# A normalised block of x made from a column layout instead of TensorE turns

## The chip, the core and the metric

The kernel runs on one core of one Trainium2 chip. A core has five engines that run side by side, each through its own list of instructions in order: TensorE (PE) multiplies matrices and turns tiles, VectorE (DVE) and GpSimd (POOL) do elementwise work and reductions, ScalarE (ACT) does functions of one argument and copies, SyncE (SP) issues transfers. Transfers (DMAs) are issued from the queues of SP, ACT and POOL and move data between device memory and the on-chip memory SBUF, which has 128 partitions. TensorE writes into PSUM, eight banks of 128 partitions by 512 float32. The metric is the device time of the whole program in microseconds (us); lower is better.

## The reference

x is 2048 tokens by 512 features, float32. It is normalised per token, and two branches start from the normalised xn: attention with 32 heads of 16, and a gated feed-forward network of width 1792.

```python
m = mean(x, axis=-1); v = var(x, axis=-1)
xn = (x - m) / sqrt(v + 1e-5)
q, k, v = split(xn @ wqkv)                    # 32 heads of 16
s = merge(softmax(q @ k.T * 16**-0.5) @ v) @ wo
f = (silu(xn @ w_gate) * (xn @ w_up)) @ w_down
out = x + s * silu(f)
```

Mean and variance belong to a token, that is, to a row of x. The products with wqkv, w_gate and w_up sum over features, and TensorE sums over partitions, so xn is needed with its features on the partitions and its tokens along the row.

## The kernel before

The tokens are worked in four blocks of TB = 512 (b = 0 to 3), each of NT = 4 tiles of 128 tokens; the features are DT = 4 chunks of 128. Float32 products are made from two halves: a tile is split into a high half, rounded to the matmul's type, and a low half, the remainder, and a product is high x high + low x high + high x low. So a tile of a projection is 12 matmuls: 4 chunks by 3 products.

The program has a prologue and a main part. The prologue makes xn in halves (`xt`, two buffers, used in turn by even and odd blocks), projects q, k and v for all tokens, and stores them in device memory (`q_d`, `k_d`, `v_d`), with the halves of xn (`xt_d`). The main part reads them back and runs attention and the feed-forward network as one stream of matmuls, their order laid out ahead of time by a planner (`plan`), then the output projection. There is no synchronisation between the parts but the data itself.

The order of the prologue is written out by hand: a loop over b, and in it over 12 tiles of projections, n = 0 to 11 (L765 to L869). Block 0 starts with the four value tiles (`value_tile`, one for 128 tokens) and goes on with the eight feature tiles (`feature_tile`, one for 128 features of q or k); the other blocks do the feature tiles first. Around each tile the loop issues what other engines are to do meanwhile for the next block. Instructions of one engine run in the order in which the loop issues them, so an instruction that waits holds up all that stand behind it on its engine.

What the change touches:

- `load_x` (L542) loads the next block of x, four transfers on SP of 128 tokens each, into `xin`, which is the tile `facc` of the main part. It is issued at n = 2 in block 0 and at n = 1 later.
- `stats` (L607) makes mean and variance of one tile of 128 tokens on DVE, tokens on the partitions. `rates` (L617) makes 1/sqrt(v + eps) for four tiles: a square root on ACT, and small DVE instructions that end with L628. They are issued behind the tiles n = 2 to 5.
- `norm` (L630) makes xn of a tile with one DVE instruction, at n = 6 to 9.
- `turn_x` (L652) turns it, at n = 7 to 10: four transposes on TensorE (L638) into the PSUM bank `acc` or `extra`, a cast on ACT to the high half (L647), a subtraction on DVE for the low half (L650). Behind the fourth tile, POOL issues two transfers of 1 MB that store the halves in `xt_d` (L656).

What runs beside it in the same steps: each feature tile has a square (L722) and a cast (L723) on ACT, a subtraction on DVE (L724), a running maximum on DVE outside block 0 (L728) and a store of 512 KB on SP (L726), with four buffers for its PSUM bank and four for its halves. In steps 3 to 18 ACT also copies parts of block 0's halves for the main part (L763). In block 0 the weights of the projections still arrive: a load on SP five tiles ahead (L565), a cast on ACT two tiles ahead (L573), a subtraction on POOL right after (L577). Each tile of block 0 needs its weights' halves.

Of the kernel before, what the change touches and what calls it, by code (L numbers as in the profile page):

```python
# [9 lines left out]
F32 = mybir.dt.float32  # L10
# [9 lines left out]
P = 128  # L20
# [5 lines left out]
NB = 4  # L26
TB = S // NB
NT = TB // P
DT = D // P
# [87 lines left out]


@with_exitstack
def tile_block(ctx: ExitStack, tc: tile.TileContext, x, wqkv, wo, w_gate, w_up, w_down, out):  # L120
    nc = tc.nc
    ctx.enter_context(tc.manual_schedule())
    x, out = x[0], out[0]
    mm, act, dve, sp, pool = nc.tensor.matmul, nc.scalar.activation, nc.vector, nc.sync, nc.gpsimd

    dram = ctx.enter_context(tc.tile_pool(name="dram", bufs=1, space=DRAM))
# [4 lines left out]
    xt_d = dram.tile([NB, 2, P, DT, TB], F32, name="xt_d")  # L131
    g_d = dram.tile([S, D], F32, name="g_d")
    o_d = dram.tile([DT, NB, P, TB], F32, name="o_d")
    s_d = dram.tile([1, TB], F32, name="s_d")

    const = ctx.enter_context(tc.tile_pool(name="const", bufs=1))
    one = ctx.enter_context(tc.tile_pool(name="one", bufs=1))
# [3 lines left out]
    ident = const.tile([P, P], F32, name="ident")  # L141
# [188 lines left out]
    rows = [slice(t * P, (t + 1) * P) for t in range(S // P)]  # L330
# [179 lines left out]
    begin, n = [], 0  # L510
# [10 lines left out]
    with ExitStack() as pro:  # L521
        pc = pro.enter_context(tc.tile_pool(name="pc", bufs=1))
# [6 lines left out]
        extra = pex.tile([P, 512], F32, name="extra")  # L529
        turns = acc, extra  # L530

        xin = facc
        wide = [slice(i * D // 2, (i + 1) * D // 2) for i in range(2)]

        def load_tile(t):
            if t:
                sp.dma_start(xin[:, t % NT], x[t * P:(t + 1) * P])
            else:
                for engine, w in zip((nc.scalar, sp), wide):
                    engine.dma_start(xin[:, t, w], x[t * P:(t + 1) * P, w])  # L540

        def load_x(b):  # L542
            for t in range(NT):
                load_tile(b * NT + t)

        load_tile(0)
        busy = pc.tile([P, P], F32, name="busy")
        dve.memset(busy, 0.0)
# [54 lines left out]
        rs = pc.tile([P, NT], F32, name="rs")  # L603
        nw = pc.tile([P, NT], F32, name="nw")
        xn = {}

        def stats(t):  # L607
            st = p2.tile([P, 2, dve.BN_STATS_DIM], F32, tag="st", name="st")
            if t or xn:
                dve.bn_stats(st[:, 0], xin[:, t])  # L610
                dve.bn_aggr(mv[:, t], st[:, 0])
            else:
                for i, w in enumerate(wide):
                    dve.bn_stats(st[:, i], xin[:, t, w])
                dve.bn_aggr(mv[:, t], st)

        def rates(first, last):  # L617
            r, n = (i[:, first:last] for i in (rs, nw))
            act(n, mv[:, first:last, 1], AF.Sqrt, bias=root, scale=4.0)
# [3 lines left out]
            dve.reciprocal(r, n)  # L623
            for t in range(first, last):
                h, n1, v1 = (i[:, t:t + 1] for i in (rs, nw, ve))
                dve.tensor_scalar(n1, v1, h, h, op0=ALU.mult, op1=ALU.mult)
            for w in cols:
                dve.scalar_tensor_tensor(rs[:, w], nw[:, w], 3.0, rs[:, w], op0=ALU.add, op1=ALU.mult)  # L628

        def norm(t, columns=(slice(0, D),)):  # L630
            xn[t] = two.tile([P, D], F32, tag="ga", name="xn")
            for w in columns:
                made = dve.tensor_scalar(xn[t][:, w], xin[:, t, w], mv[:, t, 0:1], rs[:, t:t + 1],
                                         op0=ALU.subtract, op1=ALU.mult)
            return made
# [15 lines left out]

        def turn_x(b, t, between=None):  # L652
            split_x(b, t, turn(t), between)
            if t == NT - 1 and b:
                for j in range(2):
                    pool.dma_start(xt_d[b, j], xt[b % 2][j].bitcast(F32))  # L656


        def project(pairs, xh, xl, tokens, order=None, ps=None):
# [98 lines left out]
        def copy_fx(i):  # L758
# [3 lines left out]
            dst = fx[halves[h], j].rearrange("p (c u) t -> u p c t", u=2)[u]  # L762
            nc.scalar.copy(dst[:, 2 * w:2 * w + 2], xt[0][j][halves[u], 2 * w:2 * w + 2])  # L763

        for b in range(NB):  # L765
            more = b + 1 < NB
            slots = [(feature_tile, m) for m in range(8)]
            slots = [(value_tile, t) for t in range(NT)] + slots if b == 0 else slots + [(value_tile, t) for t in range(NT)]
            for n, (make, i) in enumerate(slots):
                if b == 0:  # L770
                    if n + 5 < 12:
                        load_w(worder[n + 5])
                    if n >= 2 and n + 2 < 12:
                        high_w(worder[n + 2])
                        low_w(worder[n + 2])
                if n == (1 if b else 2) and more:
                    load_x(b + 1)
                if b == 2 and n in (6, 7):
                    load_gu(n - 6)
                if b == 2 and n == 8:  # L780
                    load_wd(0)
                if not more and n == 2:
                    split_gu(0)
                    dve.memset(acc, 0.0)
                if not more and n in (1, 3):
                    load_k(0, n // 2)
                if not more and n == 5:
                    load_q(0)
                if not more and n == 6:
                    for c in range(2):  # L790
                        load_v(0, c)
                if b == 0 and n == 1:
                    norm(2)
                    norm(3)
                if more and 6 <= n < 10:
                    norm(n - 6)
                made = make(b, i)
                if not more and n == 8:

                    for m in range(8):  # L800
                        squares(m, top[m])
                    for j in range(2):
                        dve.reduce_max(peak[:, j:j + 1], banks[j], axis=AX.X)
                    dve.tensor_add(sm, peak[:, 0:1], peak[:, 1:2])
                if b == 0 and n == 2:
                    split_x(0, 0, xf)
                if b < 2 and 0 <= 12 * b + n - 3 < 16:
                    copy_fx(12 * b + n - 3)
                if b == 0 and n == 11:
                    ring(0, 2, one)  # L810
                    queries(0, one)
                    for h in range(2):
                        pool.memset(qst[0][h * HALF:h * HALF + 2].bitcast(F32), 0.0)
                if more:
                    for t in range(NT):
                        if n == 2 + (t if b else t // 2):
                            stats(t)
                    if n == (5 if b else 4):
                        rates(0, NT)
                    if 7 <= n < 11:  # L820
                        turn_x(b + 1, n - 7)
                if not more and n == 9:
                    tops = pps.tile([P, 512], F32, tag="ps", name="tops")
                    nc.tensor.transpose(tops[0:1, :P], sm, ident)
# [4 lines left out]
                    sp.dma_start(s_d, shift.bitcast(F32))  # L829
                    for h in range(2):  # L830
                        sp.dma_start(qst[0][h * HALF:h * HALF + 1].bitcast(F32), shift.bitcast(F32)[:, None].to_broadcast([1, 2, 512]))
                    pool.dma_start(sh_d[:NG * NB].rearrange("u (j t) -> (u j) t", t=TB), s_d.to_broadcast([NG * NB * 4, TB]))
# [41 lines left out]
    late = ctx.enter_context(tc.tile_pool(name="late", bufs=1))  # L874
# [17 lines left out]
    for u in range(units):  # L892
        g, b = divmod(u, NB)
        q = qst[u % 2]
        kt = 0
        for now in range(begin[u], begin[u + 1]):
# [10 lines left out]
            for n in range(2 * size):  # L907
                t, j = tiles[n // 2], n % 2
# [61 lines left out]
    hi = two.tile([P, 2, D], F32R, tag="guh", name="rh")[:, 0]  # L970
# [74 lines left out]
```

## Time and profile before

| | |
|---|---|
| median of 3 runs | 1388.42 us (1388.14 to 1388.64) |
| the profiled execution | 1388.19 us, its span 1386.4 us |
| TensorE (PE) | 1379.9 us busy, 11197 matmuls |
| ScalarE (ACT) | 1156.8 us busy |
| VectorE (DVE) | 769.4 us busy |
| GpSimd (POOL) | 103.8 us busy |
| moved by DMAs | 151.58 MB, 109 GB/s over the span |
| the prologue | about the first 156 us of the span |

The profile is that of one execution. Its span runs from the first to the last instruction; the profiled execution's own time is 1.79 us longer. A row of a timeline gives start and duration in us, engine, line of the kernel, operation, and what is written from what, in shapes of partitions by elements; "x4" says that four instructions of the kind were merged, and a bracket gives the idle time ahead and what ended it. SPq and ACTq are the queues that issue DMAs. PEld is TensorE's load of stationary operands, which overlaps with matmuls. Matmuls are pipelined: the duration of one is longer than the distance to the next, so what a matmul costs is read from the starts. A row of groups gives line, engine, operation, count, then busy us and mean ns. A row of stretches gives the stretch, its length, the busy time of PE, PEld, DVE, ACT and POOL, the granted TensorE clock (1.00 is full), the busy share of the DMA engines and GB/s.

### The profile page before, as it was taken

Reading aid. Unit: us, or ns where it says so; the run is one execution under the profiler, and the core shown is the slowest. Engines: PE = TensorE matmul, PEld = TensorE weight load, DVE = VectorE, ACT = ScalarE, POOL = GpSimd, SP = SyncE. Lnnn points to the kernel's source line nnn. Section 1 sums busy time; section 2 is a strip of 40 time slices with the busy share of each in tenths; the row PEclk is TensorE's granted clock in tenths of the full one; section 3 lists DMA queues with packets and bytes.
Section 4 is the critical chain, followed back from the end, with each engine's and each line's share of the span. In section 5 each row is a group of like instructions: output and inputs, shape, how many; then the busy total and the mean of one; then the engine's idle time right before and its main releaser. Section 6 shows DMA issues by size and latency. Waiting matters only on the chain.

```text
span 1386.4 us, 27709 instructions
## 1 busy us (share of the span) xinstructions
PE 1379.9 (100%) x11197; PEld 871.9 (63%) x11197; DVE 769.4 (55%) x1240; ACT 1156.8 (83%) x1941; POOL 103.8 (7%) x145
## 2 busy tenths in 40 slices
PE   9999999999999999999999999999999999999998
PEld 7888666556566655665556555666566656556555
DVE  6644466355646664465465743655456545655656
ACT  6733588888989898889998988888898888899875
POOL 4200100000010000000110000000100000000142
PEclk9999999999999999999999999999999999999999
DMA  7778541124463511233723402256333312234752
GB/s 238 263 251 264 151 116 44 35 70 113 100 137 82 135 43 36 51 80 94 169 62 104 114 19 51 74 127 137 86 82 78 102 27 61 59 85 134 226 188 85
DMA packets 130981, 151.58 MB, mean 109 GB/s; under 512 B 13505, under 2 KB 83137, under 8 KB 130078
## 3 DMA queue, kind: packets, MB, share of 16 engines
q1 hardware_dynamic: 123534, 124.89, 35.1%
q0 software_dynamic: 6880, 24.32, 5.1%
q8 instruction: 90, 1.47, 0.5%
q10 hardware_dynamic: 432, 0.52, 0.1%
q14 instruction: 45, 0.37, 0.1%
HBM read 107.46 MB, written 40.11 MB: 106 GB/s over the span
## 4 chain that ended last, share of the span: by engine, by line
PE 88%; DVE 0%; DVEq 0%; issue 0%
PE acc L449 33%; PE bankx L243 30%; PE score L928 10%; PE single L928 8%; PE banky L243 6%; PE spare L928 1%; PE spare L983 0%; PE banky L983 0%; PE single L983 0%; DVE y L990 0%; PE score L983 0%; DVE y L996 0%; DVEq L1041 0%
## 5 line engine op out<-in xcount | busy, mean ns | idle before, releaser
L449 PE MATMUL acc<-pr,vst 128*17 128x512 f32 x4096 | 459.3, 593 | 0.0
L938 ACT ACTIVATE pr<-single 128x512 f32<-128x512 f32 x762 | 429.4, 604 | 17.2 <-PE single L928 0.5
L931 ACT ACTIVATE pr<-score 128x1024 f32<-128x1024 f32 x318 | 328.0, 1031 | 87.1 <-PE score L928 84.4
L449 PEld LDWEIGHTS acc<-pr,vst 128*17 128x17 f32 x4096 | 115.5, 97 | 279.5 <-issue 275.2
L243 PE MATMUL banky<-fx,guh 64*128 64x512 f32 x896 | 290.8, 392 | 0.0
L243 PE MATMUL bankx<-fx,guh 64*128 64x512 f32 x896 | 290.4, 391 | 0.1
L935 DVE COPY pr<-spare 128x512 f32<-128x512 f32 x194 | 134.2, 691 | 182.9 <-PE spare L928 163.5
L928 PE MATMUL score<-qst,kst 50*128 50x512 f32 x830 | 219.0, 418 | 0.0
L928 PE MATMUL single<-qst,kst 50*128 50x512 f32 x922 | 212.6, 398 | 0.0
L243 PE MATMUL banky<-wd,hh 64*128 64x512 f32 x672 | 196.0, 392 | 0.0
L243 PE MATMUL bankx<-wd,hh 64*128 64x512 f32 x672 | 196.0, 391 | 0.0
L948 ACT ACTIVATE pr<-pr 128x512 f32<-128x512 f32 x354 | 193.4, 641 | 0.0
L243 PEld LDWEIGHTS bankx<-fx,guh 64*128 64x128 f32 x896 | 166.8, 186 | 21.6 <-DVE guh L204 0.6
L243 PE MATMUL bankx<-fx,gul 64*128 64x512 f32 x448 | 175.6, 392 | 0.0
L243 PE MATMUL banky<-fx,gul 64*128 64x512 f32 x448 | 175.5, 392 | 0.0
L928 PEld LDWEIGHTS score<-qst,kst 50*128 50x128 f32 x830 | 98.8, 184 | 112.7 <-ACT pr L938 68.4
L243 PEld LDWEIGHTS banky<-fx,guh 64*128 64x128 f32 x896 | 166.9, 186 | 0.5
L938 ACT ACTIVATE pr<-score 128x512 f32<-128x512 f32 x194 | 116.9, 603 | 35.5 <-PE spare L928 27.5
L935 DVE COPY pr<-single 128x512 f32<-128x512 f32 x160 | 110.5, 691 | 59.9 <-PE single L928 44.1
L243 PEld LDWEIGHTS bankx<-wd,hh 64*128 64x128 f32 x672 | 125.1, 186 | 17.9
L928 PEld LDWEIGHTS single<-qst,kst 50*128 50x128 f32 x922 | 115.0, 184 | 23.4 <-ACT pr L938 7.7
L243 PEld LDWEIGHTS banky<-wd,hh 64*128 64x128 f32 x672 | 125.1, 186 | 5.2
(183 smaller groups left out, 1687.1 us busy)
## 6 DMA issues: line engine op xcount, KB each, us to landing
gur<-in_B_w_gate_dram SPq DMA_DIRECT2D x56, 256.0 KB
gur<-in_B_w_up_dram SPq DMA_DIRECT2D x56, 256.0 KB
wdr<-in_B_w_down_dram SPq DMA_DIRECT2D x56, 256.0 KB
kst<-k_d SPq DMA_DIRECT2D x192, 64.0 KB
qst<-q_d SPq DMA_DIRECT2D x192, 64.0 KB
fx<-xt_d SPq DMA_DIRECT2D x24, 512.0 KB
q_d<-parts SPq DMA_DIRECT2D x16, 512.0 KB
k_d<-parts SPq DMA_DIRECT2D x16, 512.0 KB
```

The costliest lines, as they stand in the source:

```text
L243: mm(bank, lhs[h], rhs[h], start=start, stop=stop)
L449: mm(acc[h * 32:h * 32 + DH + 1], v[:, kt % CT, h * (DH + 1):(h + 1) * (DH + 1)], probs[2 * i + h // 2][:, h % 2], start=kt == 0, stop=kt ...
L928: mm(banked[h], k[r, j, kc * P:(kc + 1) * P], q[r, j], start=True, stop=True)
L931: exps.append(act(pr, both_banks, AF.Exp, scale=0.25))
L935: dve.tensor_copy(pr[:, h], banked[h])
L938: exps.append(act(pr[:, h], banked[h], AF.Exp, scale=0.25))
L948: exps.append(act(part, part, AF.Exp, scale=0.25))
```

## The change

A second input is added: x laid out by columns, `xcols` (512 features by 2048 tokens), made on the host from x. Block 0 stays as it was. For blocks 1 to 3 the halves of xn are made from the columns, which have the features on the partitions already, so no tile is turned. Mean and rate are still made from the rows, with the tokens on the partitions, and have to be spread: TensorE turns the 128 x 8 tile of means and rates (`mr`) into 8 x 128 (`spread_mr`), ACT copies that from PSUM and issues its store to device memory (`mr_d`, 4 KB), and SP loads it back to all 128 partitions (`load_mr`, `wide_mr`, 128 x 1024, 512 KB). DVE then subtracts the mean and multiplies by the rate, both 128 x 512 with two inputs in SBUF, for each chunk of 128 features; ACT casts the high half and DVE subtracts for the low half.

The places are given per block as steps, a step being 12 b + n, in the order: load of the rows, load of the columns, statistics (two tiles a step), rates, spread, first of four steps of products; and behind the products how many steps later each chunk's low half is made. The load of `wide_mr` comes one step after the spread. `run_steps(step, 0)` stands ahead of the tile of a step, `run_steps(step, 1)` behind it: casts, low halves and the stores to `xt_d` are behind it, all else ahead. Rows and columns take a buffer each: block 1 `raw_x` (new, 8 KB per partition) and `xin`, block 2 `raw_x` for both one after the other, block 3 `xin` and `raw_x`. Rows and columns of a block are one transfer of 1 MB each.

```diff
@@ prologue
-        def load_x(b):
-            for t in range(NT):
-                load_tile(b * NT + t)
...
+        def rates_x():
+            dve.tensor_copy(mr[:, 0], mv[:, :, 0])
+            rates(0, NT)
+
+        def spread_mr(b):
+            nc.tensor.transpose(extra[:2 * NT, :P], mr.rearrange("p s t -> p (s t)"), ident)
+            nc.scalar.copy(rows_mr, extra[:2 * NT, :P])
+            nc.scalar.dma_start(mr_d[b].rearrange("s t p -> (s t) p"), rows_mr)
+
+        def load_mr(b):
+            sp.dma_start(wide_mr, mr_d[b].rearrange("s t p -> s (t p)")[None].to_broadcast([P, 2, TB]))
+
+        def columns_of(b, rows, cols, ats):
+            load, turned, counted, rated, spread, normed, lows = ats
+            block = slice(b * TB, (b + 1) * TB)
+            step(load, 0, sp.dma_start, rows, x[block].rearrange("(t p) d -> p t d", p=P))
+            step(turned, 0, sp.dma_start, cols, xcols[:, block].rearrange("(c p) t -> p c t", p=P))
+            for t in range(NT):
+                step(counted + t // 2, 0, stats, t, rows)
+            step(rated, 0, rates_x)
+            step(spread, 0, spread_mr, b)
+            step(spread + 1, 0, load_mr, b)
+            hi, lo = xt[b % 2]
+            for c in range(DT):
+                raw = cols[:, c]
+                step(normed + c, 0, dve.tensor_sub, raw, raw, wide_mr[:, 0])
+                step(normed + c, 0, dve.tensor_mul, raw, raw, wide_mr[:, 1])
+                step(normed + c, 1, nc.scalar.copy, hi[:, c], raw)
+                step(normed + lows[c], 1, dve.tensor_sub, lo[:, c], raw, hi[:, c].bitcast(F32))
+            step(normed + lows[-1], 1, store_x, b)
...
+        columns_of(1, raw_x, xin, (1, 2, 2, 4, 5, 7, (1, 2, 3, 3)))
+        columns_of(2, raw_x, raw_x, (5, 14, 12, 14, 16, 19, (1, 2, 3, 3)))
+        columns_of(3, xin, raw_x, (13, 24, 17, 24, 26, 31, (1, 2, 3, 3)))
...
-                if n == (1 if b else 2) and more:
-                    load_x(b + 1)
+                run_steps(12 * b + n, 0)
...
-                if more and 6 <= n < 10:
-                    norm(n - 6)
                 made = make(b, i)
...
-                if more:
-                    for t in range(NT):
-                        if n == 2 + (t if b else t // 2):
-                            stats(t)
-                    if n == (5 if b else 4):
-                        rates(0, NT)
-                    if 7 <= n < 11:
-                        turn_x(b + 1, n - 7)
+                run_steps(12 * b + n, 1)
@@ kernel
+        laid = [(name, a), ("A_x_columns", np.ascontiguousarray(a[0].T))] if name == "A_x" else [(name, a)]
```

More of the change, by code (lines that the diff above doesn't have):

```diff
@@ L119, in tile_block @@
 @with_exitstack
-def tile_block(ctx: ExitStack, tc: tile.TileContext, x, wqkv, wo, w_gate, w_up, w_down, out):
+def tile_block(ctx: ExitStack, tc: tile.TileContext, x, xcols, wqkv, wo, w_gate, w_up, w_down, out):
     nc = tc.nc
@@ L134, in tile_block @@
     s_d = dram.tile([1, TB], F32, name="s_d")
+    mr_d = dram.tile([NB, 2, NT, P], F32, name="mr_d")
     const = ctx.enter_context(tc.tile_pool(name="const", bufs=1))
@@ L602, in tile_block, with stats @@
         ve = pc.tile([P, NT], F32, name="ve")
-        rs = pc.tile([P, NT], F32, name="rs")
+        mr = pc.tile([P, 2, NT], F32, name="mr")
+        rs = mr[:, 1]
+        raw_x = pc.tile([P, DT, TB], F32, name="raw_x")
+        wide_mr = pc.tile([P, 2, TB], F32, name="wide_mr")
+        rows_mr = busy[:2 * NT]
         nw = pc.tile([P, NT], F32, name="nw")
         xn = {}
-        def stats(t):
+        def stats(t, src=xin):
             st = p2.tile([P, 2, dve.BN_STATS_DIM], F32, tag="st", name="st")
             if t or xn:
-                dve.bn_stats(st[:, 0], xin[:, t])
+                dve.bn_stats(st[:, 0], src[:, t])
                 dve.bn_aggr(mv[:, t], st[:, 0])
@@ L653, in turn_x, with store_x, step, run_steps @@
             split_x(b, t, turn(t), between)
-            if t == NT - 1 and b:
-                for j in range(2):
-                    pool.dma_start(xt_d[b, j], xt[b % 2][j].bitcast(F32))
+        def store_x(b):
+            for j in range(2):
+                pool.dma_start(xt_d[b, j], xt[b % 2][j].bitcast(F32))
+        steps = {}
+        def step(at, late, make, *what):
+            steps.setdefault((at, late), []).append(partial(make, *what))
+        def run_steps(at, late):
+            for make in steps.pop((at, late), ()):
+                make()
+        def rates_x():
[25 more added lines that the diff above has]
+            step(normed + lows[-1], 1, store_x, b)
         def project(pairs, xh, xl, tokens, order=None, ps=None):
@@ L1037 @@
         a = np.ascontiguousarray(a)
-        arrays[f"in_{name}_dram"] = a
-        args.append(nc.dram_tensor(f"in_{name}_dram", a.shape, mybir.dt.from_np(a.dtype), kind="ExternalInput").ap())
+        laid = [(name, a), ("A_x_columns", np.ascontiguousarray(a[0].T))] if name == "A_x" else [(name, a)]
+        for key, a in laid:
+            arrays[f"in_{key}_dram"] = a
+            args.append(nc.dram_tensor(f"in_{key}_dram", a.shape, mybir.dt.from_np(a.dtype), kind="ExternalInput").ap())
     o = nc.dram_tensor("out_0_dram", (1, S, D), F32, kind="ExternalOutput").ap()
```

## The prediction

> **What bounds the kernel now.** I read the page first, for the bound.
>
> ```profile
> span 1386.4 us, 27709 instructions
> PE 1379.9 (100%) x11197; PEld 871.9 (63%) x11197; DVE 769.4 (55%) x1240; ACT 1156.8 (83%) x1941; POOL 103.8 (7%) x145
> PEclk9999999999999999999999999999999999999999
> PE 88%; DVE 0%; DVEq 0%; issue 0%
> ```
>
> TensorE (PE) is busy from end to end at full granted clock, and the chain that ended last is PE work. A microsecond taken from PE anywhere, the prologue included, is therefore one at the end, and so is one for which PE is made to wait. Next I read the timeline of PE in block 0 (start, duration, engine, line), where a turn of x stands between two groups of matmuls, and the group view for their number.
>
> ```profile
> 30.72 0.39 PE L670 MATMUL ps<-xt,wl 128*128 128x512 f32 x1
> ...
> 31.41 0.39 PE L670 MATMUL ps<-xt,wl 128*128 128x512 f32 x1
> 31.64 0.60 PE L638 MATMUL acc<-ident,xn 128*128 128x128 f32 x4
> ...
> 32.54 0.40 PE L670 MATMUL ps<-xt,wl 128*128 128x512 f32 x1
> ```
> ```profile
> L638 PE MATMUL acc<-ident,xn 128*128 128x128 f32 x24 | 3.6, 275 | 0.0
> L638 PE MATMUL extra<-ident,xn 128*128 128x128 f32 x24 | 3.6, 272 | 0.0
> L633 DVE TENSOR_SCALAR xn<-facc,mv,rs 128x512 f32<-128x512 f32 x11 | 7.9, 722 | 0.1
> ```
>
> From one wl matmul to the next it is 0.69 us (30.72 to 31.41); with a turn between them 1.13 (31.41 to 32.54). A turn costs PE 0.44 us, though its durations add up to more: they overlap. I number the tiles of the projections as steps, 12 to a block. Their pace, from the same timeline (starts of steps 4 and 5):
>
> ```profile
> 20.50 0.62 PE L670 MATMUL ps<-xt,wh 128*128 128x512 f32 x2
> 23.28 0.64 PE L670 MATMUL ps<-xt,wh 128*128 128x512 f32 x2
> ```
>
> A step is 2.78 us of 12 matmuls, 0.23 each. PE runs through them without a wait, so a late operand is hidden only by its distance in steps.
>
> **What goes.** The 48 transposes are 12 turns: 12 x 0.44 = 5.3 us off PE. The 12 norms (L633) leave VectorE (DVE).
>
> **What comes on PE.** Three transposes of mean and rate. The nearest row is the turn of sm:
>
> ```profile
> 143.96 0.39 PE L672 MATMUL ps<-vl,xt 128*128 128x512 f32 x1
> 144.19 0.27 PE L824 MATMUL tops<-ident,sm 128*1 128x128 f32 x1
> 144.39 0.49 PE L243 MATMUL bankx<-fx,guh 64*128 64x512 f32 x1
> ```
>
> 0.20 us each, 0.6 in all. So -4.7 us, if PE waits for nothing new. It will, in five places.
>
> **Step 5, the turn of the rates.** Block 1's rates are made at step 4 and turned ahead of step 5's matmuls; PE issues in order. ScalarE (ACT), DVE and GpSimd (POOL) in turn, as they ran before; the last DVE row is block 2's, without POOL:
>
> ```profile
> 22.13 0.62 ACT L573 CAST wh<-wraw 128x512 fp32r<-128x512 f32 x1
> ...
> 25.39 0.30 ACT L619 ACTIVATE nw<-mv,root 128x4 f32<-128x4 f32 x1
> ```
> ```profile
> 25.72 0.18 DVE L623 RECIPROCAL rs<-nw 128x4 f32<-128x4 f32 x1 [0.37 <-ACT nw L619]
> 25.93 0.82 DVE L626 TENSOR_SCALAR nw<-ve,rs 128x1 f32<-128x1 f32 x4
> 26.79 0.80 DVE L628 SCALAR_TENSOR_TENSOR rs<-nw,rs 128x4 f32<-128x4 f32 x1
> ...
> 66.44 0.16 DVE L628 SCALAR_TENSOR_TENSOR rs<-nw,rs 128x4 f32<-128x4 f32 x1
> ```
> ```profile
> 22.83 1.29 POOL L577 TENSOR_TENSOR wl<-wraw,wh 128x512 fp32r<-128x512 f32 x1 [0.32 <-ACT wh L573]
> 26.27 1.29 POOL L577 TENSOR_TENSOR wl<-wraw,wh 128x512 fp32r<-128x512 f32 x1 [2.15 <-ACT wh L573]
> ```
>
> The square root now comes right behind the weight cast of step 4, at 22.7. From its start to the end of L628 it is 1.5 us with L628 at 0.16: 24.2 to 24.3, past POOL's instruction, which ends at 24.12. PE is there at 23.28. Wait: 1.0 us. The statistics before it are on time: the rows go into a buffer of their own, so their load no longer waits for the norms of block 0, as it did. Matmuls of step 5 start at 24.5, step 10 at 38.4.
>
> **Step 10, the landing of the spread rates.** SP's queue around steps 5 and 6, the trip of s_d over memory (SP's store, and POOL, which waited for it), the landing of a broadcast, and stretches whose last two columns are the DMA share and GB/s:
>
> ```profile
> 28.21 0.37 SPq L726 DMA_DIRECT2D q_d<-parts  x1
> 28.67 0.43 SPq L565 DMA_DIRECT2D wraw<-in_A_wqkv_dram  x1
> ...
> 145.55 0.34 SPq L829 DMA_DIRECT2D s_d<-shift  x1
> ```
> ```profile
> 148.93 0.56 POOL L832 DMA_DIRECT2D sh_d<-s_d  x1 [31.22 <-DMA s_d<-shift]
> ```
> ```profile
> sh_d<-s_d POOLq DMA_DIRECT2D x1, 256.0 KB, 4.2
> ```
> ```profile
> 23.00:36.00 13.00, 13.00 (x61) 10.58 (x61) 6.83 (x15) 12.31 (x20) 5.81 (x5) 1.00 0.91 287
> 46.00:58.00 12.00, 12.00 (x54) 9.72 (x53) 3.62 (x7) 8.38 (x13) 5.53 (x6) 1.00 1.03 310
> 48.00:50.00 2.00, 2.00 (x10) 1.64 (x9) 0.98 (x2) 1.93 (x3) 1.93 (x3) 1.00 0.97 398
> 50.00:58.00 8.00, 8.00 (x36) 6.47 (x35) 2.09 (x5) 5.46 (x9) 1.68 (x2) 1.00 1.05 269
> ```
>
> The load of wide_mr comes behind the store of step 5 and a weight load (28.21 and 28.67; now 1.2 later), so at 30.3. ACT's small store, issued at about 26.4, is there by then: 2 KB took 3.4 us from issue to its reader (145.55 to 148.93). Ahead of the load or beside it, from 23 us on: v_d 1088 KB, stores 2 x 512, weights 2 x 256, the rows of block 2 1024 (newly at step 5), itself 512: 4.26 MB. At 287/0.91 = 315 GB/s that ends at 36.5; with 1 us to land (an estimate, within s_d's 3.4), L = 37.5. Bounds: 34.5 if it meets an empty queue (4.2 us, the broadcast row), 39.5 if a broadcast of twice the size takes twice as long and the tail is late. I take 37.5, since the queue is full.
>
> ACT's round from one high half to the next, with a weight cast in it, and a DVE product with both inputs in SBUF, 0.61 ahead of the next instruction:
>
> ```profile
> 34.01 0.59 ACT L647 CAST xt<-acc 128x512 fp32r<-128x512 f32 x1
> 34.49 0.62 ACT L573 CAST wh<-wraw 128x512 fp32r<-128x512 f32 x1
> ...
> 37.25 0.59 ACT L647 CAST xt<-extra 128x512 fp32r<-128x512 f32 x1
> ```
> ```profile
> 501.23 0.69 DVE L237 TENSOR_TENSOR hh<-ga,hh 128x512 fp32r<-128x512 f32 x1
> 501.84 0.69 DVE L204 CAST guh<-gur 128x1024 fp32r<-128x1024 f32 x1
> ```
>
> What waits: DVE subtracts and multiplies (0.69 each), ACT casts the high half, and behind that cast, on ACT's queue, stands the weight cast of step 10. L + 1.4 + 0.5 + 0.65 = L + 2.55 = 40.05 for the weights' high half, wanted at 38.4: PE waits 1.6 us. POOL then needs 1.29 for the low half, wanted 0.47 into the step: 0.9 more with semaphores.
>
> **Step 11.** One round of ACT is 3.24 us (34.01 to 37.25), so the next low half is ready 4.56 after the last high half, wanted 4.17 after it: 0.4. If POOL first waits out one of the new DVE products it is 1.1. The rows for that are L628: 0.16 alone, 0.80 and ending at 27.59 beside a POOL instruction that ends at 27.56, so the two exclude each other. I take 1.1. [...]
>
> **Step 12, block 1 starts.** The third chunk's low half is done three rounds and 2.7 us after L (12.4), wanted at L + 11.8: 0.6 us (0.2 to 0.6).
>
> **Step 24, block 2 starts.** Here the rows of block 3, the columns of block 2 and the spread rates (2560 KB) stand where 1024 KB of x stood. xt_d starts about a microsecond after block 1's last low half (L + 13.1 = 50.6), at 51.7. From there: xt_d 2048, six stores 3072, 2560, together 7.86 MB. At the 310 GB/s of 46 to 58, the same mix: 25.4 us, and 1 to land: 78.1. Bounds 269 (81.9) and nothing (75 or less). PE reaches step 24 at 44.0 + 4.2 + 12 x 2.78 + 0.2 = 81.8 and wants the third low half 1.6 later; behind the landing DVE has 13 instructions at 0.61, 8.0 us. So all above 75.4 is a wait: 2.7 us, 0 to 6.5.
>
> **At nothing.** Block 3: its columns have step 24 to 31, its rates step 27 to 31, and four value tiles behind, in which DVE has nothing else; about 1 us is left. The 24 products (16.6 us of DVE at 0.69, against 8.7 for the norms at 0.722) lie beside PE where they aren't named above. If PE waits, ACT's casts and SP's stores behind them only move along. The attention part starts from the same data with the same distances.
>
> **Sum.** -5.3 + 0.6 + 1.0 + 1.6 + 0.9 + 1.1 + 0.6 + 2.7 = +3.2 us on the profiled execution's 1388.19 (span 1386.40 and 1.79 around it), 1391.4; the median lies 0.23 above it: 1391.6. That is 0.23%; 0.2% (2.8 us) is about what a measurement here can tell from no change.
>
> **Rivals.** Block 2's x in the trace, issued where the extra loads will be (SP), and its first reader (DVE):
>
> ```profile
> 50.15 4.15 SPq L537 DMA_DIRECT2D facc<-in_A_x_dram  x4
> ```
> ```profile
> 58.88 0.69 DVE L610 BATCH_NORM_STATS2 st<-facc 128x6 f32<-128x512 f32 x1 [3.21 <-DMA facc<-in_A_x_dram]
> ```
>
> *The second landing is hidden* (before 75.4): the first four waits remain, 5.2 against 4.7, 1388.9, no change. For it: the DMAs moved 398 GB/s from 48 to 50, and the stores are paced by PE. Against it: the first tile of x took 8.7 us (50.15 to 58.88). 0.32.
>
> *The trip fits* in block 0 as well: the queues share out so that the load lands by 33.4 and step 24 finds its data: then 4.7 less 1.0 (step 5 stays) is 3.7, 1384.7, faster. It decides at L of 35.9 for the high half, 35 for the low one. Against it: the queue's 4.26 MB. 0.10.
>
> *A long gap*: the 269 GB/s hold, PE stands still 6.5 us at step 24 in one piece: +7.0, 1395.4. 0.10. [...] No row here shows a drop: PEclk is full throughout, with no gap that long.
>
> That PE's turns are not what they cost (hidden work) is excluded by the 0.69 and 1.13.
>
> **Numbers.** The forecast has 0.48. Slower 0.58 (forecast and long gap), same 0.32, faster 0.10. Range: from 1386.0 (the trip fits, but the low halves of steps 10 and 11 are late by 0.9 and 0.4) to 1396.5 (the long gap with L later by 1.1); the forecast's own, with 0.6 to 5 us at step 24, is 1389.5 to 1394.
>
> **What would show it.** PE without L638 turns after 25 us and about 5 us less PE work; PE idle of about 1 us before step 5, released by DVE; PE or its weight load waiting for L573 and L577 at steps 10 and 11; DVE idle before the first new subtraction, released by the load of wide_mr near 37.5 and near 78; a gap at the entry of block 2. Wrong if wide_mr lands before 35.9 and 75.4, if the broadcast is far slower than its bytes, or if PE's gain is given back after the prologue.

## The result, and the profile after

The changed kernel takes 1393.74 us (median of 6 runs, 1393.63 to 1394.80), the kernel before, beside it, 1388.51 us (1388.14 to 1388.71): a ratio of 1.004, with a 95% interval of 1.003 to 1.005. It is 5.2 us slower, where 3.2 was forecast. The profiled execution took 1393.63 us.

First the page of the changed kernel, and from the view of waits all of PE's (us in total, times, the longest). The 1.1 us at the start are the kernel before's own.

```profile
span 1391.8 us, 27649 instructions
PE 1379.7 (99%) x11152; PEld 868.0 (62%) x11152; DVE 777.5 (56%) x1255; ACT 1158.7 (83%) x1944; POOL 104.3 (7%) x145
```
```profile
PE ps L712 <- ACT wh L570: 2.8, 1, 2.8
PE score L964 <- issue: 1.9, 1, 1.9
PE extra L579 <- DVE ind L586: 1.1, 1, 1.1
PE extra L674 <- DVE mr L629: 0.8, 1, 0.8
PE ps L712 <- POOL wl L574: 0.7, 1, 0.7
```

(Lines have moved: L712 and L714 are the matmuls of the projections, L570 and L574 the weights' two halves, L674 the turn of the rates, L667 everything that the steps issue, L964 the scores.) The 45 matmuls fewer are there, but PE is busy for as long as before, 1379.7 us. Most of what the missing turns should have saved went into step 10. Here is PE's timeline around it, then SP, DVE and ACT, then stretches (the seventh number after a stretch is the granted clock):

```profile
24.28 0.27 PE L674 MATMUL extra<-ident,mr 128*8 128x128 f32 x1 [0.83 <-DVE mr L629]
...
38.17 0.39 PE L712 MATMUL ps<-xt,wl 128*128 128x512 f32 x1
41.36 1.22 PE L712 MATMUL ps<-xt,wh 128*128 128x512 f32 x2 [2.80 <-ACT wh L570]
43.25 0.79 PE L712 MATMUL ps<-xt,wl 128*128 128x512 f32 x1 [0.67 <-POOL wl L574]
...
47.68 0.71 PE L712 MATMUL ps<-xt,wh 128*128 128x512 f32 x2
```
```profile
30.49 0.90 SPq L679 DMA_DIRECT2D wide_mr<-mr_d  x1
```
```profile
38.72 1.42 DVE L667 TENSOR_TENSOR facc<-facc,wide_mr 128x512 f32<-128x512 f32 x2 [6.68 <-DMA wide_mr<-mr_d]
```
```profile
40.17 0.62 ACT L667 CAST xt<-facc 128x512 fp32r<-128x512 f32 x1 [4.99 <-DVE facc L667]
40.69 0.61 ACT L570 CAST wh<-wraw 128x512 fp32r<-128x512 f32 x1
```
```profile
40.00:42.00 2.00, 0.64 (x2) 0.50 (x2) 1.97 (x4) 1.83 (x4) 0.62 (x1) 0.76 0.17 69
42.00:44.00 2.00, 1.33 (x4) 0.66 (x3) 1.75 (x4) 1.95 (x4) 1.20 (x1) 0.50 0.54 209
44.00:46.00 2.00, 2.00 (x7) 1.52 (x6) 1.53 (x3) 1.98 (x4) 1.41 (x1) 0.50 0.64 247
46.00:48.00 2.00, 2.00 (x6) 1.58 (x5) 1.97 (x4) 1.25 (x3) 0.23 (x1) 0.53 0.43 169
```

wide_mr lands at 38.72; the high half of x is cast, and right behind it the high half of step 10's weights (40.69), for which PE has stood still 2.80 us. Then PE works at half clock: a step of 12 matmuls, 2.78 us before, takes 6.32 (41.36 to 47.68). By the four stretches the clock was half for (0.24 + 0.50 + 0.50 + 0.47) x 2 / 0.5 = 6.8 us.

Two more places, the second landing with the start of block 2, and the first scores of the attention part:

```profile
77.90 1.42 DVE L667 TENSOR_TENSOR raw_x<-raw_x,wide_mr 128x512 f32<-128x512 f32 x2 [3.70 <-DMA wide_mr<-mr_d]
```
```profile
84.16 0.63 PE L712 MATMUL ps<-xt,wh 128*128 128x512 f32 x2
...
85.56 1.04 PE L712 MATMUL ps<-xt,wh 128*128 128x512 f32 x2
...
87.44 0.62 PE L712 MATMUL ps<-xt,wh 128*128 128x512 f32 x2
```
```profile
159.65 0.46 PE L964 MATMUL score<-qst,kst 50*128 50x512 f32 x1
161.97 0.47 PE L964 MATMUL score<-qst,kst 50*128 50x512 f32 x1 [1.86 <-issue]
```

Step 24 takes 3.28 us (84.16 to 87.44), 0.5 more than a step. At the scores PE stands still for 1.86 us between two matmuls that came right after one another before, "released by issue": it waits for nothing that the profile shows. So three questions were open: what the gap at the scores is, what the half clock at step 10 costs, and what the trip over memory needs.

### The profile page after: what moved, and what is told of

Its sections match the earlier page's. It is cut to its first block, busy times and chain, and to the rows that moved or that the text cites. A ratio compares the mean times of both kernels' runs of the same rounds, so it can differ in the third digit from the quotient of the medians.

```text
span 1391.8 us, 27649 instructions
## 1 busy us (share of the span) xinstructions
PE 1379.7 (99%) x11152; PEld 868.0 (62%) x11152; DVE 777.5 (56%) x1255; ACT 1158.7 (83%) x1944; POOL 104.3 (7%) x145
## 4 chain that ended last, share of the span: by engine, by line
PE 88%; issue 0%; DVE 0%; DVEq 0%
PE acc L450 32%; PE bankx L244 30%; PE score L964 10%; PE single L964 8%; PE banky L244 6%; PE spare L964 1%; PE spare L1019 0%; PE banky L1019 0%; DVE y L1026 0%; PE single L1019 0%; PE score L1019 0%; DVE y L1032 0%; DVEq L1079 0%
## 5 line engine op out<-in xcount | busy, mean ns | idle before, releaser
L964 PE MATMUL score<-qst,kst 50*128 50x512 f32 x830 | 219.1, 418 | 1.9 <-issue 1.9
L964 PE MATMUL single<-qst,kst 50*128 50x512 f32 x922 | 212.3, 398 | 0.0
L964 PEld LDWEIGHTS score<-qst,kst 50*128 50x128 f32 x830 | 98.6, 184 | 115.3 <-ACT pr L974 68.6
L964 PEld LDWEIGHTS single<-qst,kst 50*128 50x128 f32 x922 | 114.8, 184 | 23.8 <-ACT pr L974 7.8
```

The source lines that it names most:

```text
L964: mm(banked[h], k[r, j, kc * P:(kc + 1) * P], q[r, j], start=True, stop=True)
```

## The experiments

All are the changed kernel with one edit, where nothing else is said, and each was timed beside the kernel before (1388.3 to 1388.4 us).

**The gap at the scores: placement in SBUF, transfers, or code.** The first theory was placement: the two new tiles push others to new addresses.

```diff
@@ the kernel before: pad_before
+        raw_x = pc.tile([P, DT, TB], F32, name="raw_x")
+        wide_mr = pc.tile([P, 2, TB], F32, name="wide_mr")
@@ the changed kernel: late_pool
+        plater = pro.enter_context(tc.tile_pool(name="plater", bufs=1))
...
-        raw_x = pc.tile([P, DT, TB], F32, name="raw_x")
-        wide_mr = pc.tile([P, 2, TB], F32, name="wide_mr")
+        raw_x = plater.tile([P, DT, TB], F32, name="raw_x")
+        wide_mr = plater.tile([P, 2, TB], F32, name="wide_mr")
```

> The kernel before, with the two new tiles (8 KB and 4 KB a partition) allocated where the change puts them, and never used. It has all its turns and no trip. The theory of placement: the changed kernel stands still 2.2 us at the start of the attention part (first scores at 159.65 and 161.97) because 12 KB more in the prologue's pool move the tiles behind them, vt among them, under other tiles of the main part, which then wait for vt's last store. Then this kernel has that gap too: 1388.5 + 2.3 = 1390.8 us. The rival, that the gap comes from the transfers (fewer and larger ones, other queues): 1388.5 us, no gap.

> The changed kernel with its two new tiles in a pool of their own behind all others of the prologue, so that every other tile lies where it lay before. Theory of placement: the 2.2 us gap at the start of the attention part goes, 1393.7 - 2.3 = 1391.4 us. Rival, the transfers: the gap stays, 1393.7 us. Neither changes steps 5, 10 and 24.

Measured: 1388.41 us for the first (ratio 1.000, 0.9991 to 1.0009), without a gap, and 1393.74 for the second (1.0042, 1.0028 to 1.0055), with 1.8 us of PE waiting for "issue" at its scores. Placement is out. But the run with the busy gap (below) had no gap there, although it differed in PE's matmuls alone, 24 more ahead of the scores. Ahead of the attention part lies a jump, over a branch for large scores that these inputs never take. So the next edits touch only that branch.

```diff
@@ the changed kernel: never_run (inside "if fast < 1")
             with tc.tile_pool(name="gen", bufs=1) as gen:
+                for _ in range(24):
+                    mm(extra[:, :P], ident, ident, start=True, stop=True)
@@ the kernel before: never_run_before (in the same branch)
-                                ps = pps.tile([P, 512], F32, tag="ps", name="ps")
+                                if u or j == 3 or not i or j == 2 and i > 8:
+                                    ps = pps.tile([P, 512], F32, tag="ps", name="ps")
...
                                 dve.reduce_max(mx[:, i, j:j + 1], ps, axis=AX.X)
```

> The changed kernel with 24 matmuls added in the branch for large scores, which these inputs never take. Nothing that runs is changed; only the code of PE behind that branch, the attention part, lies further on, as it does in the run with the busy gap, which had the same 24 matmuls ahead of the branch and no gap at the first scores. Theory of code loading: the 2 us gap at the second score matmul, which waits for nothing that the profile shows, is PE waiting for the next piece of its program behind the jump, and whether it comes depends on where the jump lands in a piece. Then the gap goes: 1393.7 - 2.2 = 1391.5 us. Rival, a wait for data or for a store (v_d): 1393.7 us and the gap as it was.

> The kernel before with 39 matmuls taken out of the branch that is never taken (it would no longer compute the scores' maximum rightly there), so that the attention part lies about as far on in PE's program as in the changed kernel, which has 45 matmuls fewer in the prologue. Theory of code loading: a gap of about 2 us appears at the first scores, 1388.4 + 2.2 = 1390.6 us, with a prologue as in the kernel before. Rival: 1388.4 us, no gap.

Measured: 1391.27 us (1.0021, 1.0012 to 1.0030) and 1391.90 us (1.0024, 1.0014 to 1.0034). Matmuls that never run took the gap away from the changed kernel, and taking such matmuls out gave it to the kernel before. Neither edit touches a transfer, so the transfers are out as well. The timeline of PE in the first, whose two score matmuls are one row again; then, of the second, the row of the scores, and a stretch behind it:

```profile
159.85 0.70 PE L966 MATMUL score<-qst,kst 50*128 50x512 f32 x2
```
```profile
159.42 0.99 PE L929 MATMUL score<-qst,kst 50*128 50x512 f32 x2 [2.44 <-issue]
```
```profile
159.00:163.00 4.00, 3.58 (x17) 3.62 (x19) 0.00 (x0) 2.08 (x3) 1.74 (x2) 0.57 0.93 211
```

So where PE's code lies behind the jump decides whether it stands still for 1.9 to 2.4 us. In never_run_before the loss of 3.5 us is more than the gap, since the clock was half for 0.43 x 4 / 0.5 = 3.4 us behind it. Not every execution seems to have had that: two of the nine took 1390.5 us with a mean clock of 0.999, the others 1391.8 to 1392.4 with 0.998. That PE waits for a piece of its program is inferred: the view of waits names "issue" and no more (1.86 us in the changed kernel, 2.44 in never_run_before, none in never_run).

**The half clock.** Matmuls that nobody needs, in PE's gap ahead of step 10:

```diff
+                if b == 0 and n == 10:
+                    for _ in range(24):
+                        mm(extra[:, :P], ident, ident, start=True, stop=True)
                 made = make(b, i)
@@ busy_gap_12: range(12), and range(12) in the branch that is never taken, as in never_run
```

> The changed kernel with 24 matmuls of the identity (128x128, into a bank that nothing reads) ahead of step 10's first one. They do no needed work and lie in the gap of 2.8 us that is there; at 0.11 us each they take 2.6 us. Theory of the clock: it was halved because PE stood still; now it stays full, step 10's 12 matmuls take 2.8 us and the wait for the low half instead of 6.3, and since the low halves of steps 10 and 11 (POOL, ending at 43.2 and 46.2) then decide, about 2 us are won: 1391.7 us. The waits of step 11 that were forecast come back as 0.2 to 1 us. Rival, that the slow step comes from late operands or from ACT, DVE and POOL at work beside it: 1393.7 us and the matmuls of step 10 still 0.43 us apart.

> The changed kernel with 12 matmuls of the identity ahead of step 10 (24 passes in the trace at 0.11 us, 2.6 us) instead of the 24 (48 passes, 5.3 us) of the first such run, so that they fit the gap, and 12 more in the branch that is never taken, so that the attention part lies where it lay in the run without the gap at the first scores (1391.3 us, with which this one is compared). Theory of the clock: at half clock step 10 took 6.3 us; at full clock it takes 2.8 and the wait for the low half (about 1.2), and step 11 0.2 of a wait: 1.9 us won, 1389.4 us (1389.0 to 1390.0), granted clock full throughout. Rival, PE's clock is not what made step 10 slow: 1391.3 us.

Measured: 1390.41 us (1.0014, 1.0005 to 1.0023) and 1390.18 us (1.0013, 1.0004 to 1.0022). The first was sized wrongly: each of these matmuls stands in the trace as two (48 for the 24), so they took 5.3 us where the gap was 2.80 and held step 10 up; its gain is the sum of the clock and of the gap at the scores that went with it. The second is the clean one. PE's timeline, and the wait that is new:

```profile
38.50 2.84 PE L842 MATMUL extra<-ident 128*128 128x128 f32 x24
41.45 0.72 PE L712 MATMUL ps<-xt,wh 128*128 128x512 f32 x2
43.33 0.50 PE L712 MATMUL ps<-xt,wl 128*128 128x512 f32 x1 [1.16 <-POOL wl L574]
...
45.75 0.62 PE L712 MATMUL ps<-xt,wh 128*128 128x512 f32 x2
```
```profile
PE ps L712 <- DVE xt L667: 0.9, 1, 0.9
```

Operands come as late as ever (41.45), but the granted clock is 1.00 from 42 to 48, where never_run had 0.50, and step 10 takes 4.30 us (to 45.75) instead of 6.32: the clock alone cost 2.0 us there. The rival is out. At the end only 1.1 us are won against never_run: PE is earlier at step 24, while the second landing isn't, so 0.9 us of waiting for DVE's low half (L667) come back.

**The trip.** One edit takes 1 MB out of the queue ahead of wide_mr; one removes the trip and leaves all else, so that the means and rates are missing from its result; one makes the trip earlier.

```diff
@@ rows_later
-        columns_of(2, raw_x, raw_x, (5, 14, 12, 14, 16, 19, (1, 2, 3, 3)))
+        columns_of(2, raw_x, raw_x, (9, 14, 12, 14, 16, 19, (1, 2, 3, 3)))
@@ no_trip (and 24 matmuls in the branch that is never taken)
+        dve.memset(wide_mr[:, 0], 0.0)
+        dve.memset(wide_mr[:, 1], 1.0)
...
-            step(spread, 0, spread_mr, b)
-            step(spread + 1, 0, load_mr, b)
@@ best (with the edit of rows_later, and the same 24 matmuls)
-            nc.scalar.copy(rows_mr, extra[:2 * NT, :P])
-            nc.scalar.dma_start(mr_d[b].rearrange("s t p -> (s t) p"), rows_mr)
+            dve.tensor_copy(rows_mr, extra[:2 * NT, :P])
+            sp.dma_start(mr_d[b].rearrange("s t p -> (s t) p"), rows_mr)
...
-            step(spread + 1, 0, load_mr, b)
+            step(spread, 0, load_mr, b)
...
-        columns_of(1, raw_x, xin, (1, 2, 2, 4, 5, 7, (1, 2, 3, 3)))
+        columns_of(1, raw_x, xin, (1, 2, 2, 3, 5, 7, (1, 2, 3, 3)))
```

> The changed kernel with the load of block 2's rows at step 9 instead of step 5, so that 1 MB less stands ahead of the load of wide_mr; nothing else moves. Theory, a full queue: at 315 GB/s that is 3.3 us, so wide_mr lands near 35.4 instead of 38.72, step 10 starts without a gap or with one under 0.5 us, the granted clock stays full, and 2.8 us of gap and about 2 us of slow clock go: 1389 us (1388.5 to 1390). Rival, a broadcast that is slow by itself (4 KB read 128 times, 512 KB written): it lands within 0.5 us of 38.7 as before and the time stays at 1393.7 us.

> The changed kernel without the trip: means and rates of blocks 1 to 3 are left out of the result (mean 0 and rate 1 stand in wide_mr from the start), with the three transposes, their copies, stores and loads; the products, casts and loads of rows and columns stay, and the 24 matmuls in the branch that is never taken. It measures what the turns cost by themselves. Theory, 12 turns at 0.44 us with nothing that waits: 1388.4 - 5.3 = 1383.1 us (1382.8 to 1383.6). Rival, the products, the extra loads (3 MB of columns) or the locks between VectorE and GpSimd cost PE something as well: 1384 us or more, with waits of PE at steps 10 to 12 or 24.

> The changed kernel with its waits mended: the rates of block 1 at step 3 instead of 4 (no wait of 0.8 us at step 5); the turned rates copied from PSUM by DVE instead of ACT and stored and loaded by SP in the same step (the load of wide_mr near 27 instead of 30.5); block 2's rows loaded at step 9 instead of 5; and the 24 matmuls in the branch that is never taken. If bytes ahead and the place in the queues are what made it land at 38.7, wide_mr of block 1 lands at 32 to 35, ahead of the 35.9 from which step 10 waits, and only small waits at step 24 are left: 1384.0 us (1383.5 to 1385.5), against 1388.4 before. Rival, a broadcast that takes some 7 us whatever stands ahead: it lands at 35 to 36, step 10 waits under 0.5 us, 1385 to 1386 us.

Measured: 1391.62 us (1.0024, 1.0015 to 1.0033), 1382.68 us (0.9959, 0.9946 to 0.9973) and 1388.44 us (0.9998, 0.9989 to 1.0007). Without the trip PE has only the waits of the start, and 12 turns were worth 5.7 us. The other two, rows_later first (its DVE, its PE's waits behind step 5), then best (SP, DVE):

```profile
37.27 1.42 DVE L667 TENSOR_TENSOR facc<-facc,wide_mr 128x512 f32<-128x512 f32 x2 [5.29 <-DMA wide_mr<-mr_d]
```
```profile
PE score L964 <- issue: 2.0, 1, 2.0
PE ps L712 <- ACT wh L570: 1.4, 1, 1.4
PE ps L712 <- POOL wl L574: 1.2, 1, 1.2
PE ps L712 <- DVE xt L667: 1.2, 2, 1.0
```
```profile
27.25 1.36 SPq L676 DMA_DIRECT2D mr_d<-busy  x1
31.56 0.37 SPq L679 DMA_DIRECT2D wide_mr<-mr_d  x1
```
```profile
36.52 1.42 DVE L667 TENSOR_TENSOR facc<-facc,wide_mr 128x512 f32<-128x512 f32 x2 [5.27 <-DMA wide_mr<-mr_d]
```

A megabyte less ahead brings the landing from 38.72 to 37.27, 1.5 us, not the 3.3 of the bytes: neither theory's number. And 0.3 us of it is the load's earlier issue (30.18 instead of 30.49), since SP has a transfer less to issue ahead of it. PE's program is the changed kernel's, and the gap at the scores is there as well (2.0). The gap at step 10 is 1.4, as a landing at 37.27 gives by the same chain, and the clock stays full, but step 24 takes 1.2 back. In best the load was issued later than meant: SP stood 4.3 us with it (27.25 to 31.56) behind the store of 4 KB that it waits for, and in block 2 it stood 8.7 us (62.51 to 71.26). So the trip is two trips, the small store and the broadcast (5.0 us here, 8.2 in the changed kernel), each behind what is in the queues. At step 10 best has the same two waits as rows_later, but its clock was halved behind them, for 0.43 x 4 / 0.5 = 3.4 us. PE in best, then the stretch in best and in rows_later:

```profile
39.17 0.74 PE L712 MATMUL ps<-xt,wh 128*128 128x512 f32 x2 [1.38 <-ACT wh L570]
41.05 0.50 PE L712 MATMUL ps<-xt,wl 128*128 128x512 f32 x1 [1.15 <-POOL wl L574]
```
```profile
42.00:46.00 4.00, 4.00 (x13) 3.09 (x12) 3.42 (x6) 3.92 (x8) 1.62 (x1) 0.57 1.01 241
```
```profile
42.00:46.00 4.00, 4.00 (x17) 2.96 (x17) 3.49 (x7) 3.95 (x7) 1.64 (x1) 1.00 0.93 226
```

So in these two executions the length of the stops (1.38 and 1.15 us, 1.4 and 1.2 us) doesn't decide alone whether the clock falls behind them (0.57 and 1.00).

**A version without the waits.** So the trip has to be early at both ends:

```diff
@@ best2 (with 24 matmuls in the branch that is never taken, and best's copy by DVE and store by SP)
+            order = [(i, slice(0, 3)) for i in range(DT)]
+            if b == m == 0:
+                order.insert(3, (partial(spread_mr, 1), None))
-            ps = project([(wh[:, m, c], wl[:, m, c], c) for c in range(DT)], xh, xl, None)
+            ps = project([(wh[:, m, c], wl[:, m, c], c) for c in range(DT)], xh, xl, None, order)
...
             if b < NB - 1 and t == NT - 1:
-                store_v(pool, b, 0, NT)
+                step(9 if b == 0 else 12 * b + 11, 1, store_v, pool, b, 0, NT)
...
-                step(counted + t // 2, 0, stats, t, rows)
+                step(counted + (t // 2 if b > 1 else 0), 0, stats, t, rows)
...
-            step(spread, 0, spread_mr, b)
+            if b > 1:
+                step(spread, 0, spread_mr, b)
...
+        columns_of(1, raw_x, xin, (1, 2, 2, 3, 4, 7, (1, 2, 3, 3)))
+        columns_of(2, raw_x, raw_x, (8, 13, 11, 13, 14, 19, (1, 2, 3, 3)))
+        columns_of(3, xin, raw_x, (18, 24, 22, 24, 26, 31, (1, 2, 3, 3)))
@@ best3, against best2
+                step((counted + t // 3) if b == 1 else counted + t // 2, 0, stats, t, rows)
+        columns_of(2, raw_x, raw_x, (8, 13, 11, 13, 16, 19, (1, 2, 3, 3)))
@@ best4, against best3
+        columns_of(2, raw_x, raw_x, (8, 13, 11, 13, 15, 19, (1, 2, 3, 3)))
+        columns_of(3, xin, raw_x, (18, 24, 23, 24, 26, 31, (1, 2, 3, 3)))
```

> The changed kernel with the trip made early and its way cleared: all statistics of block 1 at step 2, its rates at step 3, the turn in the middle of step 4 (PE is there at 22.6, the rates are there at 21.6), the copy from PSUM by DVE and the store by SP at about 23 instead of 26.2, the load behind it; the store of block 0's values (1088 KB) moved from step 3 to step 9 and block 2's rows from step 5 to step 8, both behind the load; for block 2 rates and spread at steps 13 and 14 and for block 3 the rows at step 18, so that less stands ahead of the second load; and the 24 matmuls in the branch that is never taken. Theory: the small store takes about 4.3 us and the load about 5 behind an emptier queue, so wide_mr lands at 33 to 34, under the 35 from which steps 10 and 11 wait, and at step 24 well under 75: no new wait of PE at all, 1382.7 + 3 turns of the rates at 0.2 = 1383.3 us (1383 to 1384.5). Rival, DVE, ACT or the queues are late elsewhere (statistics of block 2 among the products of block 1, the store of block 0's values at step 9 against the later stores): waits of 1 to 3 us at steps 4, 10 to 12 or 24, 1385 to 1387 us.

> The early trip again, with its two new waits mended: three of block 1's statistics at step 2 and one at step 3 (so that block 0's low half isn't late at step 4, 0.6 us), and block 2's spread back at step 16 (its rates, made at step 13, were late for a turn at step 14: 2.0 us, and behind that gap 3.4 us at half clock, 1.7 us more). Theory: 1386.8 - 0.6 - 2.0 - 1.7 = 1382.5 us, but not under the run without the trip plus three turns, 1382.7 + 0.6 = 1383.3: 1383.3 us (1382.7 to 1384.0), with the granted clock full throughout. Rival, the second trip, two steps later, comes late for step 24 again: 1384 to 1386 us, with PE waiting for DVE's low halves at about 80.

> The early trip with the last wait mended: block 2's spread at step 15 (one step earlier than in the run before this one, where wide_mr landed at 71.7, and one later than in the run where the rates were 2.0 us late for it), and block 3's statistics from step 23 instead of 22, so that they no longer stand ahead of block 2's last low halves on DVE (1.5 us there). Theory: wide_mr of block 2 lands near 69, its last low half is made near 77, PE reaches step 24 at 76.2 and wants it at 77.8: the wait of 2.8 us goes, and with it the 3.4 us at half clock behind it (1.7 us). From the run before this one, 1387.4 - 2.8 - 1.7 = 1382.9, not under 1383.3 (the run without the trip and three turns of the rates): 1383.3 us (1383.0 to 1384.5), faster than before by 5. Rival, the bytes moved ahead keep the landing at 71: a wait of about 1 us is left, 1384 to 1386 us.

Measured: best2 1386.81 us (0.9988, 0.9979 to 0.9997), best3 1387.37 us (0.9987, 0.9978 to 0.9996), best4 1383.76 us (0.9966, 0.9952 to 0.9980). In best2 the waits at steps 5 and 10 to 12 were gone, and new ones stood at step 4 and step 14. PE's timeline there, and the stretch behind it:

```profile
51.54 0.27 PE L674 MATMUL extra<-ident,mr 128*8 128x128 f32 x1 [2.01 <-DVE mr L629]
```
```profile
52.00:56.00 4.00, 4.00 (x13) 3.09 (x12) 0.61 (x3) 0.00 (x0) 0.24 (x1) 0.58 1.03 346
```

best3 missed its number by the rival's wait, 2.6 us at step 24, and by half clock behind it (0.66 from 82 to 87, so 0.34 x 5 / 0.5 = 3.4 us of it). Its eleven executions fall into two groups, as half clock in some of them would make them: four with a mean clock of 1.000 took 1384.8 to 1385.8 us, seven with 0.998 or 0.999 took 1387.0 to 1388.2. In best4 PE waits twice behind the start, 0.7 us in all. Its load of wide_mr, its DVE at the two landings, and these waits:

```profile
26.35 0.90 SPq L679 DMA_DIRECT2D wide_mr<-mr_d  x1
```
```profile
31.95 2.40 DVE L667 TENSOR_TENSOR facc<-facc,wide_mr 128x512 f32<-128x512 f32 x2 [1.02 <-DMA wide_mr<-mr_d]
...
69.38 1.42 DVE L667 TENSOR_TENSOR raw_x<-raw_x,wide_mr 128x512 f32<-128x512 f32 x2 [0.88 <-DMA wide_mr<-mr_d]
```
```profile
PE extra L674 <- DVE mr L629: 0.7, 2, 0.5
```

The landings are at 31.95 and 69.38 instead of 38.72 and 77.90. It is 4.6 us faster than the kernel before and 10.0 faster than the changed one: 1.1 us above the run without the trip, which the three turns of the rates (forecast at 0.6) and these 0.7 us of waits cover.

## Why the prediction was right, and where it was not

The sign was right, and 1393.74 lies in the range, 2.1 us above the forecast. Term by term:

- *What goes* (-5.3): 5.7 us by the run without the trip. The prediction had PE of the kernel before run through its steps without a wait, and that was not quite so: in block 1's first step it took two matmuls 0.84 us (44.55 to 45.39) where 0.46 is usual. The run without the trip has no such stop there, and its 0.38 us are most of the difference.

```profile
44.55 1.00 PE L670 MATMUL ps<-xt,wh 128*128 128x512 f32 x2
```

- *Step 5* (1.0): 0.83 us, released by DVE's last instruction of the rates, as told.
- *Step 10, high half* (1.6): 2.80. The mechanism was right, the chain of L + 2.55 gives 41.27 for L = 38.72, and 41.36 was measured. The term mis-sized is L: the load was issued at 30.49 (30.3 forecast) but took 8.2 us, inside the bounds. The sum of the bytes ahead was a poor measure of it, as the run with 1 MB less showed.
- *Low half* (0.9) and *step 11* (1.1): in the run with full clock 1.5 us at step 10 (4.30 against 2.78) and 0.3 at step 11 (the next step begins 3.05 us later), so 1.8 against 2.0, with most of it a step earlier. In the changed kernel the slow PE hid the second. No run shows 1.1 us at step 11. That DVE and POOL exclude each other, by which the 1.1 was chosen over 0.4, was the author's estimate from the two durations of L628. What the runs show of it stands at step 10 already, where the sum had POOL's 1.29: beside DVE's second pair of products (40.65 to 42.06) POOL's subtraction took 1.81 us. In best4 the first pair of products, beside such a subtraction, took 2.40 us, where 1.42 is usual.

```profile
41.38 1.81 POOL L574 TENSOR_TENSOR wl<-wraw,wh 128x512 fp32r<-128x512 f32 x1 [6.98 <-ACT wh L570]
```

- *The half clock*: the step of the forecast that failed at step 10. The forecast looked at the clock for the long gap at step 24 alone and counted every wait of PE at its length; at step 10 the clock was 0.50 behind a wait of 2.80. It cost 2.0 us (6.32 against 4.30); the first landing as a whole cost 6.3 (2.8 + 3.5), where 4.2 was forecast.
- *Step 12* (0.6): no wait; PE came later than forecast, so its operands were there.
- *Step 24* (2.7): 0.5. The landing, 77.90, was forecast well (78.1). But PE came at 84.16 instead of 81.8, since step 10 had cost more: a later PE finds its data. In busy_gap_12, rows_later and best, in which PE came earlier, 0.9 to 1.2 us came back there.
- *The rivals*: "the second landing is hidden" asked for data before 75.4; they came at 77.90 and the wait was small all the same, for PE's own lateness. "The trip fits" needed a landing by 33.4, which only best2 to best4 reached. Of "a long gap" nothing came at step 24, where 0.5 us was lost at full clock (1.00 from 84 to 88).
- *Block 3*: at nothing, as told.
- "The attention part starts from the same data with the same distances" failed: the data were the same, the code was not. 45 matmuls fewer moved the target of a jump, which cost 2.5 us (1393.74 - 1391.27), nearly half of the 5.2. The step named the data as all that the attention part starts from, and nothing in it looked at the code.

Summed as measured: -5.7 + 0.6 (the turns, as forecast) + 0.8 + 2.8 + 3.5 (step 10 at half clock with its low half) + 0.5 + 2.5 = +5.0, against 5.2. That the forecast came as near as 2.1 us is in part luck: two terms that it lacked (clock and code, 4.5 us) stood against waits that didn't come (steps 11, 12 and 24: 4.4 forecast and, in the changed kernel, 0.5 found).

## What to carry to other kernels

Work taken off the bounding engine is won only if what replaces it is ready in time: the turns were worth 5.7 us, and the late trip and what followed from it gave back 8.2 (0.6 + 0.8 + 2.8 + 3.5 + 0.5), while the same change with its landings 7 to 8.5 us earlier, and without the gap at the scores, kept 4.6. Count a short stop of TensorE at more than its length, since half clock can stand behind it (here 2.80 us of stop and then 6.8 us at 0.50, and in best 1.38 and 1.15 us of stops and then 3.4 us at half clock). And when the number of an engine's instructions ahead of a taken branch changes (here 45 matmuls, for 2.5 us), look at the first instructions behind it before blaming data; instructions in a branch that never runs tell the two apart.

## What was not expected of the hardware

- The clock was halved after waits of PE of 2.80 us (for 6.8 us), 2.44 (for 3.4) and 2.01 us (for (1 - 0.58) x 4 / 0.5 = 3.4; there it fell at about 52.6, a microsecond after PE had gone on). In best it was halved behind waits of 1.38 and 1.15 us with two matmuls between them, and in rows_later, behind 1.4 and 1.2, it was not (0.57 and 1.00 from 42 to 46). Half clock for 3.4 us costs about 1.7, an estimate (half of the 3.4).
- Where PE's code lies behind a taken jump is worth 1.9 to 2.4 us of standing still, with nothing in the trace but "issue".
- A store of 4 KB followed by the load that waits for it held SP 4.3 and 8.7 us in blocks 1 and 2 of best. The broadcast of 512 KB took 5.0 us (best) to 8.2 us (the changed kernel) from issue to landing in block 1; a megabyte less ahead of it was worth 1.1 us of that (7.1 in rows_later).
